# GpSimd's elementwise operations cut into four pieces each, and one weight subtraction moved to VectorE, in a fused attention and mixture-of-experts kernel

## The chip, the cores and the metric

The kernel runs on one core of one Trainium2 chip. Times are device microseconds of a whole execution. The engines are called as in the profile: PE (TensorE matmul) with PEld (its weight loads), DVE (VectorE), ACT (ScalarE), POOL (GpSimd), SP (the queue that issues most transfers).

## The reference, cut to what matters

Three layers in a row, all in float32. Attention with a causal mask over 4 batches, 8 heads, 576 positions and 64 channels is mixed, by a gate per head, with a linear memory that is read through phi(q):

```
scores = scale * q @ k^T, causal;  a = softmax(scores);  local = a @ v
phi(x) = where(x > 0, x, exp(x) - 1) + 1
mem_out = (phi(q) @ M_prev) / (phi(q) . z_prev + 1e-6)
x = g * mem_out + (1 - g) * local            # 2304 tokens of 512
```

Then routing: logits = x @ w_gate, each token goes to the one of 8 experts with the largest logit, with a factor from the softmax and a second gate. Each expert is two matrix products with a relu between (512 to 1024 to 512). A gated layer ends it: sigmoid(x @ w_gate) * (x @ w_val) @ w_out with an inner width of 1536.

## The kernel before, in words

Float32 products that need care are computed from two parts, a rounded high part (`hi`, a copy by ACT into the fp32r format) and the remainder (`lo`, a subtraction by DVE or POOL), with three matmuls for one.

**Attention** (about the first 300 us) works on 16 pairs of heads, two pairs to a group, so 8 groups. Per pair: q and k are transposed by PE and split (`q_part` L303, `k_part` L314), nine query tiles of scores are made (L345), masked with the row maximum by DVE (L365), exponentiated by ACT (L375), transposed again (L410) and multiplied with v (L440). At the end of a pair DVE turns the row sums to reciprocals (`recip`, L384 and L385), `spread` (L390, on POOL or DVE) lays them out, PE broadcasts them (L398), and DVE scales and adds (L450, L455).

**phi(q)** is computed once per group on tiles of 128 x 1152: ACT's exp, then on POOL `phi_sum` in four instructions (max L258, min L260, add L262, times z L264), on DVE `phi_norm` (a sum L269 and three tiny operations to L272), and on POOL `phi_scale` (L276). `phi_sum` of the next group cannot be far ahead, as tile `e` has one buffer and `ph` two.

**Routing** follows per batch: logits (L772), transposed (L788), copied by DVE (step `r0`, L797 and L798), argmax as a one-hot matrix (`r1`, five DVE instructions L807 to L812), factors (`r2` to `r5`, L828 to L850, on DVE or POOL with an ACT step between). For the last batch a matmul counts the tokens (`p0`, L889), a chain of 14 small DVE instructions gives each token its slot (`p1`, L896 to L973), and `p3` (L940), `p4` (L990), L996, L1000 and L1003 make the token lists. Then the first tokens are gathered (`x0`, `x1`, L1006, issued by POOL), which wait for the lists, for the store of the factors (`sd`, L853, issued by SP) and for all stores of x; the experts' first product waits for the gather.

**The first weights.** Eight parts of expert 0's weights are split while attention ends: `wh` n (L1097, ACT) and `wl` n (L1102). Parts 2 to 5 have their low part on DVE, parts 0, 1, 6 and 7 on POOL. In the kernel before, part 0 has only `wh` 0 to wait for, part 1 also `r4` of the last batch, the next ones the end of routing.

**What sets the order.** A planner (class `Plan`) simulates all steps of attention and routing with fixed costs in us, for each engine, and takes the step and the engine that can start first (rank breaks ties within 0.02 us; a step that may go to one of two engines has 0.1 added for DVE and 0.05 for POOL). A step behind one on the same engine gets a lag of 0.06 to 0.13, behind one on another engine 0.15 to 0.2. The result is written out as it stands: every engine executes its own list strictly in order, and waits there for what the others owe it. The experts and the gated layer have orders of their own that the change does not touch.

Of the kernel before, what the change touches and what calls it, by code (L numbers as in the profile page):

```python
# [9 lines left out]
F32 = mybir.dt.float32  # L10
# [3 lines left out]
ALU = mybir.AluOpType  # L14
# [4 lines left out]
P = 128  # L19
B, H, S, D = 4, 8, 576, 64  # L20
HG = 4
NP = B * H // 2
NQ = 9
NK = 5
# [5 lines left out]
NT = NTOK // P  # L30
# [24 lines left out]
class Plan:  # L55
# [15 lines left out]
    def add(self, name, rank, cost, fn, needs=(), takes=(), uses=()):  # L71

        assert name not in self.steps, name
        self.steps[name] = (rank, cost, fn, tuple(needs), tuple(takes))
        for t in (*takes, *uses):
            self.users.setdefault(t, []).append(name)
# [48 lines left out]
class Attention:  # L125
# [15 lines left out]
    def constants(self, beta):  # L141
# [41 lines left out]
        for hg in range(2):  # L183
            h0 = hg * HG
            nc.vector.tensor_copy(
                self.gf[:, hg, 0:16].rearrange("p (c h) -> p c h", h=HG),
                g[:, None, h0 : h0 + HG].to_broadcast([P, 4, HG]),
            )
# [10 lines left out]
    def load_nat(self, gi, nm, l):  # L199
        b, h0 = gi // 2, (gi % 2) * HG  # L200
        src = self.q if nm == "q" else self.k
        if l == 0:
            self.G[gi, nm] = self.ld.tile([P, 18 * 64], F32, name=f"{nm}n", tag=f"{nm}n")
        t = self.G[gi, nm]
        tv = t[:, 0:1024].rearrange("p (c h d) -> p c h d", c=4, d=64)
        for hh in (2 * l, 2 * l + 1):
            self.nc.sync.dma_start(
                out=tv[:, :, hh, :], in_=src[b, h0 + hh, 0:512, :].rearrange("(c p) d -> p c d", p=P)
            )
        self.nc.sync.dma_start(  # L210
            out=t[l * 64 : (l + 1) * 64, 1024:1152].rearrange("p (h d) -> p h d", d=64),
            in_=src[b, h0 + 2 * l : h0 + 2 * l + 2, 512:576, :].rearrange("h p d -> p h d"),
        )

    def load_z(self, gi):
        b, h0 = gi // 2, (gi % 2) * HG
        self.G[gi, "z"] = zf = self.ld.tile([P, 18 * 64], F32, name="zf", tag="zf", bufs=1)
        z1 = self.z[b, h0 : h0 + HG].rearrange("h d -> (h d)")
        for c in range(4):
            self.nc.sync.dma_start(out=zf[:, c * 256 : (c + 1) * 256], in_=z1.partition_broadcast(P))  # L220
        for l in range(2):
            self.nc.sync.dma_start(
                out=zf[l * 64 : (l + 1) * 64, 1024:1152],
                in_=z1[l * 128 : (l + 1) * 128].partition_broadcast(64),
            )
# [27 lines left out]
        self.nc.scalar.activation(self.G[gi, "e"], self.G[gi, "q"], AF.Exp)  # L253

    def phi_sum(self, gi, n):
        nc, q, ph, e = self.nc, self.G[gi, "q"], self.G[gi, "ph"], self.G[gi, "e"]
        if n == 0:
            nc.gpsimd.tensor_scalar(ph, q, 0.0, None, ALU.max)  # L258
        elif n == 1:
            nc.gpsimd.tensor_scalar(e, e, 1.0, None, ALU.min)  # L260
        elif n == 2:
            nc.gpsimd.tensor_tensor(ph, ph, e, ALU.add)  # L262
        else:
            nc.gpsimd.tensor_tensor(e, ph, self.G[gi, "z"], ALU.mult)  # L264

    def phi_norm(self, gi):
        nc = self.nc
# [5 lines left out]

    def phi_scale(self, gi):
        pv = self.G[gi, "ph"].rearrange("p (a d) -> p a d", d=64)
        self.nc.gpsimd.tensor_tensor(pv, pv, self.G[gi, "nm"][:, :, None].to_broadcast([P, 18, 64]), ALU.mult)  # L276


    GROUPS = ((0, 1, 2), (3, 4))
# [178 lines left out]
    def run(self, ex, change):  # L458
# [8 lines left out]
        add = p.add  # L467
# [8 lines left out]

        for gi in range(NP * 2 // HG):
            u0 = gi * NQ * (HG // 2)
            r = u0 - 18
            for l in range(2):  # L480
                for i, nm in enumerate("qk"):
                    add(("L", nm, gi, l), r + 2 * l + i, {"SP": 1.6}, lambda e, a=(gi, nm, l): self.load_nat(*a),
                        needs=[("L", nm, gi, 0)] * l, takes=[] if l else [(nm + "n", gi)], uses=[(nm + "n", gi)] * l)
# [7 lines left out]
            for n, c in enumerate((3.06, 3.06, 2.57, 2.57)):  # L491
                needs = [("L", "q", gi, 1)] if n == 0 else [("phe", gi)] if n == 1 else [("phs", gi, n - 1), ("phs", gi, 0)]
# [6 lines left out]

        for pi in range(NP):  # L500
            gi, u0 = pi // 2, pi * NQ
            before = [("S", u, si) for u in range(u0 - 2 * NQ, u0 - NQ) if u >= 0 for si in range(len(self.spans(ORDER[u % NQ])))]
            for g in range(2):
                n = (384, 192)[g]
                r = u0 - 13 + g
                for nm in "qk":
                    kz = nm == "k" and g == 0
                    add(("X", nm, pi, g), r, {"PE": PO + n / 1200}, lambda e, a=(nm, pi, g): self.turn(*a),
                        needs=[("L", nm, gi, pi % 2)] + (before if nm == "q" else [("X", "k", pi, 0)] if g else []),
                        takes=[("T", (nm, pi, g))] + ([("kz", pi)] if kz else []), uses=[(nm + "n", gi)])  # L510
                for j in range(2):
                    add(("qh", pi, g, j), r, {"AC": ac(n)}, lambda e, a=(pi, g, j, 0): self.q_part(*a),
                        needs=[("X", "q", pi, g)], uses=[("T", ("q", pi, g))])
                    add(("ql", pi, g, j), r, {"DV": dv(n)}, lambda e, a=(pi, g, j, 1): self.q_part(*a),
                        needs=[("qh", pi, g, j)], uses=[("T", ("q", pi, g))])
                add(("kh", pi, g), r, {"AC": ac(n)}, lambda e, a=(pi, g, 0): self.k_part(*a),
                    needs=[("X", "k", pi, g)] + ([("kh", pi, 0)] if g else []), uses=[("T", ("k", pi, g)), ("kz", pi)])
# [4 lines left out]
                    needs=[("ph", gi)] + ([("X", "ph", pi, 0)] if g else []),  # L522
                    takes=[("T", ("ph", pi, g))] + ([] if g else [("phT", pi)]), uses=[("ph", gi)])
                add(("pp", pi, g), r, {"AC": ac(n), "DV": dv(n)}, lambda e, a=(pi, g): self.p_part(e, *a),
                    needs=[("X", "ph", pi, g)] + ([("pp", pi, 0)] if g else []),
                    uses=[("T", ("ph", pi, g)), ("phT", pi)])
            kept = {}
            for n_ in range(NQ):
                u, t = u0 + n_, ORDER[n_]
                n, two = 64 * (t + 1), (pi, n_ // 2)  # L530
                sp = self.spans(t)
                for si, (k0, k1) in enumerate(sp):
                    gs = range(1 if k1 <= 384 else 2)
                    needs = [("kl", pi, g) for g in gs] + [("ql", pi, 0 if t < 6 else 1, j) for j in range(2)]
                    needs += [("S", u, 0)] if si else [("S", u - 1, len(self.spans(ORDER[(u - 1) % NQ])) - 1)] if u else []
                    add(("S", u, si), u, {"PE": PO + max(0.21 + (k1 - k0) / 2400, 3 * (k1 - k0) / 2400)}, lambda e, a=(u, si): self.scores(*a),
                        needs=needs, takes=[("Sp", (u, si))], uses=[("kz", pi)])
                    takes = [("mx", u)] + ([("Sm", two)] if n_ % 2 == 0 else []) + ([("sums", pi)] if n_ == 0 else []) if si == 0 else []
                    needs = [("S", u, si)] + ([("m", u, 0)] if si else [("m", u - 1, 0)] if n_ else [])
# [8 lines left out]
                for chunks in ([list(range(min(nb, 4)))] + ([[4]] if nb == 5 else [])):  # L548
                    f = chunks[0]
                    add(("t", u, f), u + 2, {"PE": PO + 0.107 * len(chunks)}, lambda e, a=(u, tuple(chunks)): self.turn_probs(*a),  # L550
                        needs=[("e", u), *before], takes=[("T", (u, f))], uses=[("Sm", two)])
                    for c0, c1 in ((f, min(chunks[-1] + 1, full)), (max(f, full), chunks[-1] + 1)):
                        if c0 < c1:
                            w = (c1 - c0) * 128
                            add(("v", u, c0), u + 2 + 0.1, {"AC": ac(w), "DV": dv(w)},
                                lambda e, a=(u, c0, c1, f): self.keep_probs(e, *a),
                                needs=[("t", u, f)], uses=[("T", (u, f))])
# [5 lines left out]
            for bk in range(2):  # L563
# [4 lines left out]
                    needs=[("b", pi, bk)] + ([("bc", pi, 0)] if bk else []),  # L568
                    takes=[] if bk else [("rb", pi)], uses=[("T", ("b", pi, bk))] + ([("rb", pi)] if bk else []))
            for bk in range(2):  # L570
                r = u0 + 22 + bk
                last = (2, 4)[bk]
                for i in range(last + 1):
                    needs = [("o", pi, bk, i - 1)] if i else [("L", "v", gi)]
                    needs += [k for t in range(9) if t >= 2 * i and (t <= 4 if bk == 0 else t >= 4) for k in kept[t]]
                    n = 288 - max(0, i * 128 - bk * 288)
# [3 lines left out]
                    needs=[("pp", pi, 0), ("pp", pi, 1), ("L", "M", gi), ("o", pi, bk, last)],  # L580
                    takes=[("O", ("m", pi, bk))], uses=[("MB", gi), ("phT", pi)])
                b, hp = divmod(pi, H // 2)
                first = hp == 0 and bk == 0
                add(("os", pi, bk), r + 0.5, {"DV": dv(288)}, lambda e, a=(pi, bk): self.out_scale(*a),
                    needs=[("o", pi, bk, last), ("bc", pi, bk)] + ([] if first else [("os", 4 * b, 0)]),
                    takes=[("xT", b)] if first else [], uses=[("O", (pi, bk)), ("rb", pi)] + ([] if first else [("xT", b)]))
                add(("oc", pi, bk), r + 0.5, {"DV": dv(288)}, lambda e, a=(pi, bk): self.out_add(*a),
                    needs=[("os", pi, bk), ("om", pi, bk)], uses=[("O", ("m", pi, bk)), ("xT", b)])
# [8 lines left out]
        for n, tag in enumerate(("qn", "kn", "zf", "e")):  # L597
            add(("w", 4 + n), 999, {"SP": 1.5}, lambda e, n=n: ex.load_part(self.spare(n)), needs=[("w", 3 + n), ("phs", NP * 2 // HG - 1, 3)],
                takes=[(tag, "w")])
# [6 lines left out]
        wide = [n for n in p.steps if n[0] in ("phn", "qh", "ql", "S", "m", "r", "D", "b", "t", "v", "o")]  # L606
        for n in range(8):
            add(("wh", n), 900 + n, {"AC": 0.95}, lambda e: ex.split_hi(),
                needs=[("w", 7), ("lc", B - 1, 1), *wide] + ([("wh", n - 1)] if n else []) + [("xc", NT - 1 if n else NT - 4)])
            late = [] if n < 1 else [("r4", B - 1)] if n < 2 else ["places"] if n < 5 else ["x1"]  # L610
            add(("wl", n), 900 + n, {"DV": 1.14} if n in (2, 3, 4, 5) else {"PL": 2.3},
                lambda e, n=n: ex.split_lo(n, self.nc.vector if e == "DV" else self.nc.gpsimd), needs=[("wh", n)] + late)
        for n in range(2):
            add(("f", n), 998, {"SP": 1.0}, lambda e: ex.load_part(), needs=[("wl", n)] + ([("f", n - 1)] if n else []))
        add("ahead", 999, {"SP": 3.0}, lambda e: ex.load_ahead(self.gather), needs=["x1"] + [("wl", n) for n in range(4)])
# [396 lines left out]
class Experts:  # L1012
# [84 lines left out]
        self.nc.scalar.activation(hi, t, AF.Copy)  # L1097
        self.half[n] = t, hi, lo, slot

    def split_lo(self, n, eng):  # L1100
        t, hi, lo, slot = self.half.pop(n)
        eng.tensor_tensor(lo, t, hi.bitcast(F32), ALU.subtract)  # L1102
        if slot is not None:
            self.free.append(slot)

# [579 lines left out]
```

## Time and profile before

| | us |
|---|---|
| median of 3 runs | 1127.98 |
| lowest and highest | 1125.14, 1132.57 |
| the profiled execution | 1123.5 |
| its span | 1121.7 |
| PE, PEld busy, share of the span | 92%, 80% |
| DVE, ACT, POOL busy, share of the span | 49%, 42%, 26% |

The profile describes the one execution of 1123.5 us; 1.8 us of it lie around the span. Attention fills the span to about 300 us, routing and the first gather reach to about 322, experts to about 640, the gated layer the rest.

### The profile page before, as it was taken

The numbers are of one execution on the slowest core, as the hardware profiler recorded it, in microseconds if no ns is written. First come the engines' busy times: TensorE is split into PE (matmuls) and PEld (weight loads), VectorE is DVE, ScalarE is ACT, GpSimd is POOL, SyncE is SP. The second block draws the span as 40 slices with busy tenths as digits, with TensorE's granted clock in tenths as the row PEclk, the third lists the DMA queues.
The fourth block names the chain that finished last, engine by engine and source line by source line (L and its number), as shares of the span: only waits on it lengthen the run. The fifth ranks groups of instructions, "written<-read, shape, count | busy, mean of one in ns | idle before, by whom it ended". The sixth has DMA issues, their size and how long they took to land. (4 is left out here: it accounts for less than half of the span.)

```text
span 1121.7 us, 16871 instructions
## 1 busy us (share of the span) xinstructions
PE 1037.1 (92%) x6133; PEld 900.6 (80%) x6133; DVE 545.5 (49%) x1232; ACT 466.5 (42%) x1074; POOL 293.8 (26%) x287
## 2 busy tenths in 40 slices
PE   6998998999869799979987679999999999999997
PEld 5766776777559689968976579999899999999996
DVE  6888867767585153227225699941212111121112
ACT  5875776777545252126214365521212211221211
POOL 7667245333265152025114300000110100100101
PEclk9999999999979999989998989999999999999999
DMA  5646433322268264128224466500010100100000
GB/s 119 140 103 175 83 85 85 97 61 58 66 196 291 75 210 159 38 72 280 87 62 137 141 188 197 177 12 1 29 57 1 47 10 1 58 1 1 29 1 29
DMA packets 111899, 102.50 MB, mean 91 GB/s; under 512 B 69520, under 2 KB 86928, under 8 KB 111760
## 3 DMA queue, kind: packets, MB, share of 16 engines
q1 hardware_dynamic: 107888, 88.18, 26.8%
q0 software_dynamic: 3872, 12.62, 3.7%
q8 instruction: 69, 1.13, 0.5%
q14 instruction: 70, 0.57, 0.2%
HBM read 84.49 MB, written 16.28 MB: 90 GB/s over the span
## 5 line engine op out<-in xcount | busy, mean ns | idle before, releaser
L1482 DVE TENSOR_TENSOR G<-G,pT 128x384 f32<-128x384 f32 (+1 forms) x74 | 40.1, 543 | 248.7 <-PE pT L1468 248.5
L1514 POOL DMA_INDIRECT out_dram<-o,rows x18 | 17.5, 971 | 462.7 <-ACT o L1510 213.5
L345 PE MATMUL Sp<-kz,qz 128*128 128x288 f32 (+8 forms) x480 | 100.3, 340 | 7.6 <-DVE mx L365 7.6
L1489 ACT ACTIVATE Gh<-G 128x384 fp32r<-128x384 f32 (+1 forms) x74 | 38.2, 516 | 162.3 <-DVE G L1482 162.1
L1478 ACT ACTIVATE G<-pH 128x384 f32<-128x384 f32 x72 | 35.4, 491 | 129.9 <-PE pH L1468 129.8
L345 PEld LDWEIGHTS Sp<-kz,qz 128*128 128x128 f32 x480 | 73.9, 197 | 17.0 <-DVE mx L365 9.5
L375 ACT ACTIVATE Sm<-Sm,mx 128x576 f32<-128x576 f32 (+2 forms) x144 | 79.8, 557 | 16.3 <-DVE mx L365 16.0
L1102 POOL TENSOR_TENSOR W<-raw,W 128x1024 fp32r<-128x1024 f32 x23 | 60.5, 2632 | 76.5 <-ACT W L1097 76.4
L365 DVE CUSTOM_DVE_ANT_0 Sm<-Sp,mask 128x288 f32<-128x288 f32 (+2 forms) x144 | 63.4, 450 | 18.8 <-PE Sp L345 12.4
L1499 PE MATMUL pX<-W,Gh 128*128 128x512 f32 x220 | 68.9, 394 | 0.0
L1097 ACT ACTIVATE W<-raw 128x1024 fp32r<-128x1024 f32 x60 | 61.7, 1054 | 16.9 <-DMA y_dram<-y 8.4
L283 ACT ACTIVATE pt<-T 64x128 f32<-64x128 f32 (+4 forms) x159 | 53.6, 368 | 31.9 <-PE T L410 28.2
L410 PE MATMUL T<-ident,Sm 128*128 128x128 f32 (+1 forms) x400 | 61.6, 281 | 5.0 <-ACT pt L283 3.4
L440 PE MATMUL O<-pt,vn 128*64 128x288 f32 (+4 forms) x512 | 59.5, 352 | 0.0
L1102 DVE TENSOR_TENSOR W<-raw,W 128x1024 fp32r<-128x1024 f32 x37 | 55.0, 1497 | 7.1 <-ACT W L1097 7.1
L1487 DVE TENSOR_TENSOR Gl<-G,Gh 128x384 fp32r<-128x384 f32 (+1 forms) x74 | 40.4, 546 | 33.9 <-ACT Gh L1489 33.9
L410 PEld LDWEIGHTS T<-ident,Sm 128*128 128x128 f32 (+1 forms) x400 | 43.3, 136 | 16.5 <-ACT pt L283 5.1
L1233 PE MATMUL pH<-W,xh 128*128 128x512 f32 x80 | 28.4, 501 | 28.3 <-issue 28.1
L1468 PE MATMUL pT<-xh,W 128*128 128x384 f32 x264 | 52.5, 342 | 0.0
L1468 PE MATMUL pT<-yh,W 128*128 128x384 f32 x264 | 51.3, 336 | 0.0
L440 PEld LDWEIGHTS O<-pt,vn 128*64 128x64 f32 (+1 forms) x512 | 30.4, 137 | 23.6 <-issue 11.2
L1468 PE MATMUL pH<-yh,W 128*128 128x384 f32 x240 | 46.9, 337 | 1.4 <-DVE xl L1457 1.4
(325 smaller groups left out, 2459.5 us busy)
## 6 DMA issues: line engine op xcount, KB each, us to landing
raw<-in_moe_w_dram SPq DMA_DIRECT2D x60, 512.0 KB, 4.9
raw<-in_moe_w_gate_dram SPq DMA_DIRECT2D x12, 512.0 KB, 4.3
raw<-in_moe_w_val_dram SPq DMA_DIRECT2D x12, 512.0 KB, 3.7
raw<-in_moe_w_out_dram SPq DMA_DIRECT2D x12, 512.0 KB, 3.3
y_dram<-y SPq DMA_DIRECT2D x9, 513.0 KB, 3.1
qn<-in_q_dram SPq DMA_DIRECT2D x32, 128.0 KB, 2.8
kn<-in_k_dram SPq DMA_DIRECT2D x32, 128.0 KB, 2.7
zf<-in_z_prev_dram SPq DMA_DIRECT2D x32, 128.0 KB, 5.8
```

Of the source, the lines that this page charges most:

```text
L283: self.nc.scalar.activation(out, in_, AF.Copy)
L345: nc.tensor.matmul(Sp[:, 0 : k1 - k0], lhsT=z[:, a, t, :], rhs=kz[:, c, k0:k1], start=(p_ == 0), stop=(p_ == 2))
L365: self.nc.vector.tensor_tensor_reduce(out=self.Sm[u][:, k0:k1], in0=self.Sp[u, si][:, 0 : k1 - k0], in1=self.mask[:, 512 - 64 * t + k0 : 5 ...
L375: self.nc.scalar.activation(self.Sm[u], self.Sm[u], AF.Exp, scale=-1.0, bias=self.mx[u][:, si : si + 1], accum_out=self.sums[pi][:, ORDER[ ...
L410: nc.tensor.transpose(T[:kr, n * 128 : (n + 1) * 128], self.Sm[u][:, i * 128 : i * 128 + kr], self.ident)
L440: nc.tensor.matmul(O[j * 64 : (j + 1) * 64, q0 - q0b : 288], lhsT=self.G[gi, "v"][:kr, i, 2 * l + j, :], rhs=PT[:kr, j, i, q0:q1], start=( ...
L1097: self.nc.scalar.activation(hi, t, AF.Copy)
L1102: eng.tensor_tensor(lo, t, hi.bitcast(F32), ALU.subtract)
L1468: nc.tensor.matmul(t, lhsT=w[:, k * P : (k + 1) * P], rhs=x[:, k, :], start=(m == k == 0), stop=(m == 2 and k == 3),)
L1482: nc.vector.tensor_tensor(t, t, p, ALU.mult)
L1487: nc.vector.tensor_tensor(l, t, hi.bitcast(F32), ALU.subtract)
L1499: nc.tensor.matmul(po[g][jj], lhsT=a[:, ts], rhs=w, start=(f == 0 and m == 0), stop=(f == NF - 1 and m == 2), skip_group_check=True,)
```

## The change

The four instructions of `phi_sum` and the one of `phi_scale` are issued as four each, over 320, 320, 256 and 256 of the 1152 columns. `wl` 1, on POOL, is issued as four instructions of 256 columns. `wl` 0 goes from POOL to DVE, in one instruction. `wh` 0 no longer names the last logits copy as a need. The planner's costs for all of these but `wl` 0 (2.3 on POOL before, 1.14 on DVE after) stay as they were. `wl` 6 and 7 and the experts' splits stay whole.

```
+PIECES = ((0, 5), (5, 10), (10, 14), (14, 18))
 def phi_sum(self, gi, n):
-    nc, q, ph, e = self.nc, self.G[gi, "q"], self.G[gi, "ph"], self.G[gi, "e"]
-    if n == 0:
-        nc.gpsimd.tensor_scalar(ph, q, 0.0, None, ALU.max)
...
+    for a, b in PIECES:
+        q, ph, e = (self.G[gi, nm][:, a * 64 : b * 64] for nm in ("q", "ph", "e"))
+        if n == 0:
+            nc.gpsimd.tensor_scalar(ph, q, 0.0, None, ALU.max)
+        elif n == 1:
+            nc.gpsimd.tensor_scalar(e, e, 1.0, None, ALU.min)
+        elif n == 2:
+            nc.gpsimd.tensor_tensor(ph, ph, e, ALU.add)
+        else:
+            nc.gpsimd.tensor_tensor(e, ph, self.G[gi, "z"][:, a * 64 : b * 64], ALU.mult)
 def phi_scale(self, gi):
-    self.nc.gpsimd.tensor_tensor(pv, pv, self.G[gi, "nm"][:, :, None].to_broadcast([P, 18, 64]), ALU.mult)
+    for a, b in PIECES:
+        nm = self.G[gi, "nm"][:, a:b, None].to_broadcast([P, b - a, 64])
+        self.nc.gpsimd.tensor_tensor(pv[:, a:b], pv[:, a:b], nm, ALU.mult)
 # Attention.run
-    needs=[("w", 7), ("lc", B - 1, 1), *wide] + ([("wh", n - 1)] if n else []) + [("xc", NT - 1 if n else NT - 4)])
+    needs=[("w", 7), *wide] + [("lc", B - 1, 1)] * (n > 0) + ([("wh", n - 1)] if n else []) + [("xc", NT - 1 if n else NT - 4)])
-    add(("wl", n), 900 + n, {"DV": 1.14} if n in (2, 3, 4, 5) else {"PL": 2.3},
-        lambda e, n=n: ex.split_lo(n, self.nc.vector if e == "DV" else self.nc.gpsimd), needs=[("wh", n)] + late)
+    add(("wl", n), 900 + n, {"DV": 1.14} if n in (0, 2, 3, 4, 5) else {"PL": 2.3},
+        lambda e, n=n: ex.split_lo(n, *((self.nc.vector, 1) if e == "DV" else (self.nc.gpsimd, 4 if n < 2 else 1))), needs=[("wh", n)] + late)
-def split_lo(self, n, eng):
+def split_lo(self, n, eng, parts=1):
     t, hi, lo, slot = self.half.pop(n)
-    eng.tensor_tensor(lo, t, hi.bitcast(F32), ALU.subtract)
+    w = 1024 // parts
+    for o in range(0, 1024, w):
+        eng.tensor_tensor(lo[:, o : o + w], t[:, o : o + w], hi.bitcast(F32)[:, o : o + w], ALU.subtract)
```

## Rows read from the trace of the kernel before

**Rows 1.** Windows: stretch, length, busy us by engine, clock, DMA share, GB/s.
```profile
38.00:46.00 8.00, 6.83 (x49) 5.06 (x50) 7.13 (x17) 5.14 (x18) 7.13 (x3) 1.00 0.66 143
62.00:72.00 10.00, 7.83 (x50) 5.95 (x47) 6.10 (x12) 4.84 (x17) 6.85 (x5) 0.83 0.35 83
82.00:88.00 6.00, 4.72 (x38) 3.65 (x35) 5.19 (x9) 3.31 (x10) 6.00 (x2) 1.00 0.78 146
106.00:120.00 14.00, 10.02 (x63) 7.85 (x61) 13.42 (x33) 6.76 (x20) 9.47 (x4) 0.88 0.29 97
180.00:192.00 12.00, 8.42 (x50) 6.76 (x48) 11.67 (x27) 5.37 (x17) 8.24 (x3) 0.86 0.21 68
```

**Rows 2.** Three source lines: min/median/max ns, first and last start.
```profile
L384 DVE TENSOR_SCALAR rc<-sums,iog x16: 223/230/3044, 26.2 to 285.6; 128x9 f32<-128x9 f32 x16
...
L390 DVE TENSOR_TENSOR dg<-rows,rc x2: 3056/3221/3386, 62.0 to 82.2; 128x576 f32<-128x576 f32 x2
...
L844 DVE TENSOR_SCALAR r_a<-r_a x2: 1395/1464/1534, 114.1 to 187.0; 128x4 f32<-128x4 f32 x1, 128x5 f32<-128x5 f32 x1
```

**Rows 3.** Timeline of DVE and POOL, 106 to 114: start, us, instruction.
```profile
107.07 3.12 POOL L260 TENSOR_SCALAR e<-e 128x1152 f32<-128x1152 f32 x1
...
107.39 2.64 DVE L812 TENSOR_TENSOR O<-r_t,r_vm 128x32 fp32r<-128x32 f32 x1
...
110.27 0.18 DVE L828 TENSOR_TENSOR r_d<-L,r_mx 128x32 f32<-128x32 f32 x1
110.28 2.65 POOL L262 TENSOR_TENSOR ph<-ph,e 128x1152 f32<-128x1152 f32 x1
...
110.37 2.61 DVE L832 TENSOR_TENSOR r_sel<-O,L 128x32 f32<-128x32 f32 x1
```

**Rows 4.** Timeline of POOL, 84 to 95: the instruction behind an L258.
```profile
84.84 3.39 POOL L260 TENSOR_SCALAR e<-e 128x1152 f32<-128x1152 f32 x1
```

**Rows 5.** Groups of POOL instructions by form: busy, mean ns, idle before.
```profile
L258 POOL TENSOR_SCALAR ph<-qn 128x1152 f32<-128x1152 f32 x8 | 25.0, 3127 | 6.9 <-PE T L299 5.1 <-DMA MB<-in_M_prev_dram 1.8
L262 POOL TENSOR_TENSOR ph<-ph,e 128x1152 f32<-128x1152 f32 x8 | 21.1, 2640 | 0.4
...
L276 POOL TENSOR_TENSOR ph<-ph,nm 128x1152 f32<-128x1152 f32 x8 | 17.0, 2120 | 30.6 <-DVE nm L272 19.6 <-DVE mx L365 7.4 <-DMA vn<-in_v_dram 3.6
L390 POOL TENSOR_TENSOR dg<-rows,rc 128x576 f32<-128x576 f32 x14 | 16.1, 1153 | 72.5 <-PE T L398 55.3 <-DVE pt L285 8.8 <-DVE rb L285 3.3
L940 POOL TENSOR_SCALAR Bm<-col,rf,tok 128x128 fp32r<-128x128 f32 x8 | 6.2, 794 | 1.1 <-DVE sid L850 1.1
...
L844 POOL TENSOR_SCALAR r_d<-r_d 128x5 f32<-128x5 f32 x1 | 0.3, 279 | 0.1
```

**Rows 6.** Timeline of DVE: the first and the fourth sum of `phi_norm`.
```profile
31.98 1.35 DVE L269 TENSOR_REDUCE nm<-e 128x18 f32<-128x1152 f32 x1
...
97.38 1.35 DVE L269 TENSOR_REDUCE nm<-e 128x18 f32<-128x1152 f32 x1
```

**Rows 7.** Timeline of all engines, routing of the last batch to the gather.
```profile
301.32 2.35 POOL L1102 TENSOR_TENSOR W<-raw,W 128x1024 fp32r<-128x1024 f32 x1 [12.33 <-ACT W L1097]
301.35 2.38 DVE L808 TENSOR_TENSOR r_t<-L,r_mx 128x40 f32<-128x40 f32 x1
...
304.23 0.23 DVE L812 TENSOR_TENSOR O<-r_t,r_vm 128x40 fp32r<-128x40 f32 x1
...
305.06 0.45 DVE L896 TENSOR_TENSOR_SCAN inc<-seg,T 128x144 f32<-128x144 f32 x1
...
306.84 2.33 DVE L915 CAST ranki<-rank 128x18 int32<-128x18 f32 x1
...
310.61 0.37 SPq L853 DMA_DIRECT2D x_dram<-sid  x1
...
314.26 1.12 POOL L1006 DMA_INDIRECT xn<-x_dram,kept  x1 [5.13 <-DVE starts L983]
...
335.79 1.21 DVE L1102 TENSOR_TENSOR W<-raw,W 128x1024 fp32r<-128x1024 f32 x1
```

More of the change, by code (lines that the diff above doesn't have):

```diff
@@ L255, in phi_sum @@
     def phi_sum(self, gi, n):
-        nc, q, ph, e = self.nc, self.G[gi, "q"], self.G[gi, "ph"], self.G[gi, "e"]
-        if n == 0:
-            nc.gpsimd.tensor_scalar(ph, q, 0.0, None, ALU.max)
[L259 to L264, printed above, removed]
+        nc = self.nc
+        for a, b in PIECES:
[8 more added lines that the diff above has]
+                nc.gpsimd.tensor_tensor(e, ph, self.G[gi, "z"][:, a * 64 : b * 64], ALU.mult)
     def phi_norm(self, gi):
```

## The prediction, on record before the change was run

> **What bounds the kernel now.** The page's busy times come first: PE is busy 92% of the span (table above), so time is to be gained only where PE has nothing to do or runs at its low clock. The windows show where in attention that is. In five stretches, 50 us together, PE is busy 6.83 of 8, 7.83 of 10, 4.72 of 6, 10.02 of 14 and 8.42 of 12 us [rows 1]: 1.17, 2.17, 1.28, 3.98 and 3.58, in sum 12.2 us idle. In the same stretches DVE and POOL are both nearly full. In the second, fourth and fifth the granted clock is 0.83, 0.88 and 0.86 of full speed on average [rows 1]; what is missing, times the length, is 1.7 us each, 5.1 us. Part of that fell while PE had no work; I take 4 as lost. So 16.2 us of attention are at stake.
>
> The source lines and the timeline then say what DVE does there. A reciprocal's first step that takes 0.23 us at the median took 3.04 once, and both outlays on DVE took over 3 us [rows 2], although the same 128x576 product takes the slower POOL 1.15 [rows 5]. At 107.39 a product of 32 columns takes 2.64 us; POOL's 3.12 us operation runs from 107.07 [rows 3]. The DVE operation ends at 110.03, POOL's at 110.19. At 110.28 the next POOL operation begins, and the DVE operation at 110.37 takes 2.61 and ends at 112.98, POOL's at 112.93. So a DVE operation with two SBUF inputs, or a plain one from SBUF to SBUF, stands still until POOL's running operation is about done, and all that is queued behind it on DVE (masks, copies out of PSUM) with it; PE runs dry after 1 to 3 us. In routing the same happens twice on the path to the first gather: 2.38 us at 301.35 and 2.33 at 306.84 for operations of 40 and 18 columns [rows 7], where a sibling takes 0.23 [rows 7].
>
> **The change, part by part.** *Pieces against the stalls.* What a DVE operation waits for becomes one piece, if it is let in between two pieces. The rows say it is: L812 got in between two POOL operations of which the second reads what the first wrote [rows 3]; the outlay of 82.19 (3.06 us, ends 85.25) got in between L258 and L260, which don't depend on each other, and L260 took 3.39 instead of 3.12 [rows 2, 4]. A tensor_tensor piece of 320 columns is some 0.25 + 320 x 2.1 ns = 0.9 us, so a wait is at most about 0.9, and lowest nothing. The lone stalls (38 to 46, 62 to 72, 82 to 88) waited 2.8, 2.7 and 2.4 us (3.04 less 0.23; 3.39 and 3.06 less some 0.7 of their own) and left PE idle for 1.17, 2.17 and 1.28 [rows 1, 2]: PE bridged 1.6, 0.5 and 1.1. With at most 0.9 of waiting only the second can leave something; of 4.6 us I take 4.4 as gone. The stretches at 106 and 180 hold a chain of eight such operations each (r1 to r4 of a batch). In the first the three long waits (2.64, 2.61 and 1.53 less 0.2 each) sum to 6.2 us against 3.98 idle [rows 1 to 3], so PE bridges some 2.2; the other, with 3.58 idle, holds the other long L844 [rows 2] and is taken as its like. With pieces each waits between 0.3 (half of a piece, when POOL streams at all) and 0.75; I take 0.5, for the row of L828, which slipped through without waiting while L832 behind it waited [rows 3]: 8 x 0.5 = 4, less 2.2, leaves 1.8 idle each, 3.6 together (0.4 to 7.6 by the ends). The clock fell after idle times of 2.17 and more and did not after 1.28 [rows 1], so the 4 us come back. Of 16.2 us this leaves 12.4.
>
> *What pieces cost POOL.* Each added instruction costs POOL its fixed part. A tensor_scalar of 5 columns takes 0.28 [rows 5]; the form with two per-row scalars at 128 columns takes 0.79, which less 128 x 2.5 ns is 0.47. Below, 0.15, since two products of 576 and 1152 columns (1.15 and 2.12) extrapolate to 0.19 at none and neighbours overlap a little. I take 0.25, nearest to the plain form. Fifteen more per group are 3.75 us (2.3 to 7.0), 30 us over eight groups. Eight groups spread over 300 us, and the first four phi_norms lie within 65 [rows 6], so the later groups have more room, and POOL's idle time takes it in (19.6 of the 30.6 us before L276 are waits for DVE, and 72.5 us lie before the outlays [rows 5]). Before 100 us it matters: from one phi_norm to the next POOL owes L276, two tensor_scalars, two tensor_tensors and an outlay, 2.12 + 2 x 3.13 + 2 x 2.64 + 1.15 = 14.8 [rows 5], and DVE about 2.1 with latencies 0.3: 17.2 us. The first and the fourth phi_norm are 65.4 us apart [rows 6], 21.8 each; with 3.75 more the chain is 20.95, so the fourth comes at best 2.6 us earlier, while the lone stalls give back 4.4 plus some 1.3 of clock by then. DVE, in order, waits at phi_norm for the rest, with masks and copies behind it; PE bridges about half: 1.5 us off. Attention gains 10.9.
> [...]
>
> *The first weights' low part.* The planner's list, followed by hand with its costs: `wh` 0 starts as before (the logits copy it no longer names is long done), so `wl` 0 can start when `r1` ends, 0.13 before DVE could do `r2` and before the counts are there. It goes on DVE between `r1` and `p1`, 1.21 us [rows 7]. POOL, now empty, gets `r2`, and later `r4` and `wl` 1 behind it. On the chip: L808 loses 2.18, so L812's end moves from 304.46 to about 302.3; `wl` 0 fills DVE to 303.5; L896 starts 1.5 us earlier than 305.06 and L915 runs free (2.1 more): `p1` is 3.6 earlier. But `r2` on POOL waits for `wl` 0's reads, `r3` stands behind a `wh` more on ACT, and `r4` ends near 308, so the factors' store goes at about 308.4 against 310.61. Then `wl` 1 in four pieces (2.35 + 3 x 0.25) occupies POOL to about 312, with the gather behind it: 312 against 314.26. 2.2 us gained; bounds 4.3 (both stalls) and -1 (POOL's factor steps later still). SP gains no instruction; the second raw load, tied to `wl` 1, goes some 1 us later, and is for expert 1, which is split only beside expert 0's products. The `wh` edit alone costs nothing.
>
> The sum is 10.9 + 2.2 = 13.1: 1110.4 against the profiled 1123.5. That execution was 4.5 faster than the median shown; from the median it is **1115**.
>
> **The rivals.** *Blocked in turn (0.22).* Each of the eight chained operations waits for a whole piece, 8 x 0.8 = 6.4, as much as before. The chains keep their idle time and clock; the lone stalls give 5.7, less 1.5, routing 2.2: 6.4 us, 1122. For it speaks L832, held at once by the next POOL operation; against it that L828 passed [rows 3].
> [...]
> *POOL sets the early pace (0.16).* With 0.35 us and more per added instruction the chain is 22.5 us, and nothing of the first 100 us is gained: 13.1 less 4.2, 8.9 us, 1119. For it speaks the 0.79 us row, against it the 0.28 one.
> *Slower (0.06).* The same chain at 0.7 us per added instruction: 27.7 against 21.8, three times, 17.7 us late at the fourth phi_norm, against 8.9 from the chains and routing: 1137. It turns from gain to loss at about 0.5 (24.7, 8.7 us late); no row has so high a fixed part.
> *Not what stretches them (0.06).* The long DVE operations wait for something else, and pieces change nothing: 1128. Their ends within 0.2 us of POOL's speak against it.
>
> **How the numbers follow.** The forecast has 0.50; its own range is 1109 to 1120. This kernel's timing tells no change below about 1%, 11.3 us. Faster by that: most of the forecast (0.44) and a quarter of the early-pace case (0.04), 0.48; slower 0.06; within it 0.46. The range is 1106 (all idle and clock back, both stalls of routing, the median's spread) to 1124 (blocked in turn with nothing from routing).
>
> **What would show it.** The windows at 106 and 180 with PE idle under 2 us and full clock; L384 and the outlays on DVE under 1.2 us; L812 and L832 under 1. Spacing of POOL's pieces tells the fixed part, 0.25 or more; phi_norm's fourth sum near 95. One L1102 on DVE right behind L812 near 302.3, the gather near 312 less what attention gained. Wrong if chained operations each take a piece's time, if DVE stands idle before L269, or if the gather stands behind the factors' store.

## The result, and the profile after

The changed kernel takes **1113.35 us** (median of six runs, 1111.45 to 1114.58) against 1128.41 (1125.14 to 1132.57) for the kernel before in the same runs: ratio 0.9861, 95% interval 0.9838 to 0.9884. It is 1.4% faster. The forecast was 1115 in a range of 1106 to 1124, with faster by over 1% as its likeliest sign. Line numbers from phi(q) on are 3 to 7 higher than before (L384 is L389, L390 is L395, L812 is L817, L1006 is L1011).

The profiled execution after is the slowest of its six (1114.58), the one before (1123.5) lies below all six of its own. So the two traces differ by only 8.9 us of span. The marks in the traces say where they part:

| us from the span's start | before | after | gained since the mark above |
|---|---|---|---|
| last tokens of x complete (first of the eight last x transposes, L868, now L873) | 298.52 | 288.33 | 10.19 |
| first gather (L1006, now L1011) | 314.26 | 301.93 | 2.14 |
| first transposes of the gated layer (L1450, now L1457) | 644.3 | 631.8 | 0.2 |
| end | 1121.7 | 1112.8 | -3.6 |

The last row lies in a layer that the change doesn't touch; the last section returns to it. Attention and the way to the gather gave 12.3 us; both had been put close to that (10.9 and 2.2).

The page's busy times of the kernel after:
```profile
PE 1038.6 (93%) x6133; PEld 903.0 (81%) x6133; DVE 521.3 (47%) x1229; ACT 466.6 (42%) x1074; POOL 312.8 (28%) x415
```
POOL is busy for more of the span (28%, before 26%). The windows of attention, columns as in [rows 1]:
```profile
20.00:30.00 10.00, 8.49 (x52) 7.34 (x49) 6.69 (x24) 8.10 (x27) 7.94 (x11) 0.83 0.64 146
38.00:46.00 8.00, 7.97 (x58) 5.76 (x55) 5.92 (x20) 6.07 (x21) 8.00 (x10) 1.00 0.81 146
62.00:72.00 10.00, 10.00 (x75) 7.70 (x71) 6.16 (x20) 7.86 (x24) 10.00 (x14) 1.00 0.58 121
82.00:88.00 6.00, 6.00 (x42) 4.61 (x41) 5.41 (x18) 4.65 (x15) 6.00 (x8) 1.00 0.92 229
100.00:120.00 20.00, 15.70 (x97) 13.46 (x96) 11.46 (x47) 10.94 (x34) 12.61 (x16) 0.83 0.60 156
172.00:180.00 8.00, 8.00 (x62) 7.19 (x61) 7.07 (x30) 5.81 (x16) 7.98 (x10) 1.00 0.34 114
180.00:192.00 12.00, 12.00 (x89) 9.41 (x88) 9.60 (x30) 9.97 (x31) 7.48 (x11) 1.00 0.54 139
```
The three stretches with lone stalls [rows 1] are full and at full clock, though POOL has not a free moment in them. So is the second chain, which now runs from 174 to 180. Of these stretches only 20 to 30 and the one around 106 have PE idle and the clock down, the latter with 4.3 of 20 us idle.

The DVE operations that had been held [rows 2, 3], min/median/max ns in the kernel after:
```profile
L389 DVE TENSOR_SCALAR rc<-sums,iog x16: 222/230/850, 27.4 to 275.4; 128x9 f32<-128x9 f32 x16
...
L395 DVE TENSOR_TENSOR dg<-rows,rc x2: 753/754/755, 61.6 to 78.1; 128x576 f32<-128x576 f32 x2
...
L849 DVE TENSOR_SCALAR r_a<-r_a x2: 183/318/454, 103.9 to 178.2; 128x4 f32<-128x4 f32 x1, 128x5 f32<-128x5 f32 x1
```
Where 3.04, 3.39 and 1.53 us stood, no operation takes over 0.85. The second chain's timeline, with POOL working without a break from 172.02 to 185.27:
```profile
174.78 0.45 DVE L813 TENSOR_TENSOR r_t<-L,r_mx 128x40 f32<-128x40 f32 x1
175.26 0.20 DVE L814 TENSOR_TENSOR r_t<-r_t,desc 128x40 f32<-128x40 f32 x1
...
175.72 0.39 DVE L817 TENSOR_TENSOR O<-r_t,r_vm 128x40 fp32r<-128x40 f32 x1
...
176.50 0.19 DVE L833 TENSOR_TENSOR r_d<-L,r_mx 128x40 f32<-128x40 f32 x1
176.61 0.46 DVE L837 TENSOR_TENSOR r_sel<-O,L 128x40 f32<-128x40 f32 x1
...
178.22 0.18 DVE L849 TENSOR_SCALAR r_a<-r_a 128x5 f32<-128x5 f32 x1
```
Each waits 0 to 0.27 us beyond its own 0.18 to 0.2, where 0.5 had been taken.

What stopped PE near 106 is another thing. Each tile of 128 tokens of x is copied out of PSUM into one of two buffers `xt`, which SP then stores. SP's queue in the kernel after:
```profile
92.00 1.75 SPq L221 DMA_DIRECT2D zf<-in_z_prev_dram  x4
...
95.03 3.56 SPq L244 DMA_DIRECT2D vn<-in_v_dram  x4
99.42 2.52 SPq L247 DMA_DIRECT2D vn<-in_v_dram  x1
102.03 1.99 SPq L235 DMA_DIRECT2D MB<-in_M_prev_dram  x2
...
104.76 0.85 SPq L888 DMA_DIRECT2D x_dram<-xt  x2
```
The copies into `xt` on ACT's timeline, the same stretch:
```profile
100.72 0.60 ACT L288 ACTIVATE xt<-T 128x512 f32<-128x512 f32 x1 [0.23 <-PE T L873]
...
101.63 0.60 ACT L288 ACTIVATE xt<-T 128x512 f32<-128x512 f32 x1
...
110.19 0.60 ACT L288 ACTIVATE xt<-T 128x512 f32<-128x512 f32 x1 [5.01 <-DMA x_dram<-xt]
```
The first two tiles are copied by 102.23, but SP issues their stores only at 104.76, behind loads for the next group; the first of these (z) could not go before 92.00, because POOL's last piece of L267 reads the old z until 91.97. The third copy finds both buffers still waiting for their stores, ACT stands for 5.01 us, and PE waits 4.30 us, from 106.55 to 110.85, for ACT's next copy. This is a new wait that none of the prediction's parts had. In the kernel before SP issues the same two stores here:
```profile
106.86 1.23 SPq L883 DMA_DIRECT2D x_dram<-xt  x2
```
There the first copy ends at 106.83, so its store goes at once. With the change the copy is 5.5 us earlier and its store only 2.1. That z's wait for POOL sets the whole delay is read from the queue's order; no run moved the z load alone.

Routing of the kernel after, as in [rows 7]:
```profile
291.86 0.23 DVE L817 TENSOR_TENSOR O<-r_t,r_vm 128x40 fp32r<-128x40 f32 x1
291.98 1.22 DVE L1109 TENSOR_TENSOR W<-raw,W 128x1024 fp32r<-128x1024 f32 x1
292.17 1.17 POOL L837 TENSOR_TENSOR r_sel<-O,L 128x40 f32<-128x40 f32 x1 [0.69 <-DVE O L817]
...
293.33 0.45 DVE L901 TENSOR_TENSOR_SCAN inc<-seg,T 128x144 f32<-128x144 f32 x1
...
295.11 0.17 DVE L920 CAST ranki<-rank 128x18 int32<-128x18 f32 x1
...
298.29 0.37 SPq L858 DMA_DIRECT2D x_dram<-sid  x1
...
298.80 2.79 POOL L1109 TENSOR_TENSOR W<-raw,W 128x256 fp32r<-128x256 f32 x4
...
301.93 1.13 POOL L1011 DMA_INDIRECT xn<-x_dram,kept  x1 [0.34 <-DVE kept L989]
```
The order is the forecast one: `wl` 0 on DVE right behind `r1`, `r2` on POOL held beside it (L837 takes 1.17 us and ends 0.14 behind `wl` 0, where another on POOL, at 243.8, takes 0.26; that it is `wl` 0's reads that hold it is not shown), the cast free (0.17 for 2.33), then the factors' store, `wl` 1 in four pieces and the gather behind it, 13.60 us after attention's mark instead of 15.74.

### The profile page after: what moved, and what is told of

Same layout as the page of the kernel before. It is cut to its first block, busy times and chain, and to the rows that moved or that the text cites. A ratio compares the mean times of both kernels' runs of the same rounds, so it can differ in the third digit from the quotient of the medians.

```text
span 1112.8 us, 17008 instructions
## 1 busy us (share of the span) xinstructions
PE 1038.6 (93%) x6133; PEld 903.0 (81%) x6133; DVE 521.3 (47%) x1229; ACT 466.6 (42%) x1074; POOL 312.8 (28%) x415
## 5 line engine op out<-in xcount | busy, mean ns | idle before, releaser
L1109 POOL TENSOR_TENSOR W<-raw,W 128x1024 fp32r<-128x1024 f32 (+1 forms) x25 | 58.6, 2349 | 64.7 <-ACT W L1102 64.6
L445 PEld LDWEIGHTS O<-pt,vn 128*64 128x64 f32 (+1 forms) x512 | 29.9, 135 | 23.5 <-issue 10.9
```

The lines of the kernel that those rows point to most:

```text
L445: nc.tensor.matmul(O[j * 64 : (j + 1) * 64, q0 - q0b : 288], lhsT=self.G[gi, "v"][:kr, i, 2 * l + j, :], rhs=PT[:kr, j, i, q0:q1], start=( ...
L1109: eng.tensor_tensor(lo[:, o : o + w], t[:, o : o + w], hi.bitcast(F32)[:, o : o + w], ALU.subtract)
```

## The experiments

All were timed in five rounds; ratios are to the kernel before in the same runs. Edits are against the changed kernel.

**e1: only `phi_sum` in pieces** (`phi_scale`, `wl` 0, `wl` 1 and `wh` 0 as before):
```
 def phi_scale(self, gi):
-    for a, b in PIECES:
+    for a, b in ((0, 18),):
 # Attention.run
-    needs=[("w", 7), *wide] + [("lc", B - 1, 1)] * (n > 0) + ...
+    needs=[("w", 7), ("lc", B - 1, 1), *wide] + ...
-    {"DV": 1.14} if n in (0, 2, 3, 4, 5) ... 4 if n < 2 else 1
+    {"DV": 1.14} if n in (2, 3, 4, 5) ... 1
```


> Only the four instructions of phi_sum are in pieces; phi_scale is whole, and the first weights are as in the kernel before. Theory (a DVE operation that needs the shared path stands still until POOL's running instruction is done): attention's gain is all here, since the long waits fell under phi_sum's instructions: the last eight transposes of x begin near 288 instead of 298.5, the two waits of over 2.1 us in routing stay, and the time is about 2 us above that of the whole change: 1116 against 1128. Rival (the consumers of phi_scale start earlier on its pieces): most of the gain is missing, 1124 or more.

Measured 1116.09 (1112.47 to 1118.76), ratio 0.9879 [0.9847, 0.9911]. The lone stalls and the second chain's are gone without the rest of the change; the gap of PE near 106 is there too (3.06 us), and so is one wait beside the whole `phi_scale` (an L389 of 1.22 us). Attention's mark is at 285.13. In routing both long operations are back, and the gather comes 16.15 us after the mark:
```profile
287.96 2.38 DVE L813 TENSOR_TENSOR r_t<-L,r_mx 128x40 f32<-128x40 f32 x1
...
293.45 2.32 DVE L920 CAST ranki<-rank 128x18 int32<-128x18 f32 x1
```

**e2: only the weights' part** (`phi_sum` and `phi_scale` whole):
```
-        for a, b in PIECES:
+        for a, b in ((0, 18),):
```


> phi_sum and phi_scale are whole; only the first weights' low parts are as in the change (part 0 on DVE, part 1 in four pieces on POOL). Theory: attention is as before, with its long waits; routing's path to the gather is 2 us shorter: about 1126, ratio 0.998. Rival (the gain of the change is routing's and what follows it): 1118 or less.

Measured 1125.55 (1122.09 to 1130.97), ratio 0.9976 [0.9954, 0.9998]. Attention is as before, with PE busy 16.01 of 20 us in 100 to 120 and 8.42 of 12 in 180 to 192. The gather comes 13.90 after attention's mark, 1.84 less than before. So the two parts add: about 12 and 3 us of the 15, and e1's and e2's intervals cover that.

**e3: a third x buffer**, to take the new wait away. The tile for every third early copy lies in a buffer that is idle until the gather:
```
-            xt = self.r2.tile([P, DM], F32, name="xt", tag="xt")
+            xt = self.xn[0][:, :DM] if j < EARLY and j % 3 == 2 else self.r2.tile([P, DM], F32, name="xt", tag="xt")
```


> The change, with a third buffer for the tiles of x that wait for their store (every third tile before the thirteenth lies in a buffer that is idle until the gather). Theory (at 105 to 110 ACT waits 5.0 us for a store of x to land, which the SP queue issued late behind the z load that waits for POOL's last product, and this takes the place of the stall removed there): the wait goes, PE's idle time of 4.3 us between 100 and 120 falls under 1.5 and the low clock after it goes: 1108 to 1109, 4 to 5 us under the change. Rival (another wait is due there next, as POOL's pace sets the groups): no faster than the change by more than 1 us, 1113.

Measured 1108.63 (1100.41 to 1112.24), ratio 0.9814 [0.9776, 0.9852]. The window around 106 with this edit:
```profile
100.00:120.00 20.00, 20.00 (x149) 16.04 (x147) 16.63 (x60) 15.39 (x49) 14.26 (x19) 1.00 0.94 168
```
PE is full there, the clock never falls, and the time is the expected one. Four pieces had freed DVE here too; the gain had gone into the wait for a buffer.

**e8: the first four x stores from ACT's queue**, two buffers as before:
```
-        self.nc.sync.dma_start(out=self.x_dram[j * P : (j + 1) * P, :DM], in_=self.xt[j])
+        (self.nc.scalar if j < 4 else self.nc.sync).dma_start(out=self.x_dram[j * P : (j + 1) * P, :DM], in_=self.xt[j])
```


> The change, with the first four stores of x issued by ACT's queue right after the copies, instead of by SP, where they stand behind the loads of z, v and M. If SP's order delays them (copies done at 101.3 and 102.2, stores issued at 104.8), they go 2.5 to 3 us earlier, ACT's wait of 5.0 us falls to 2 to 3 and the time by 2 to 4 us: 1109 to 1111. If only the transfer itself is slow there (5 us to land with the DMA engines full), or ACT pays for the issues, no gain: 1113.

Measured 1105.91 (1103.08 to 1110.49), ratio 0.9808 [0.9778, 0.9839], more than expected. ACT's copy and queue in this kernel:
```profile
99.65 0.60 ACT L288 ACTIVATE xt<-T 128x512 f32<-128x512 f32 x1 [0.23 <-PE T L873]
...
101.27 0.35 ACTq L888 DMA_DIRECT2D x_dram<-xt  x1
...
105.34 0.60 ACT L288 ACTIVATE xt<-T 128x512 f32<-128x512 f32 x1 [0.21 <-DMA x_dram<-xt]
```
The first store goes 1.0 us behind the end of its copy, where SP's went 3.4 behind, and the third copy waits 0.21 instead of 5.01. So most of the wait was SP's late issue; the rest is that the store also lands sooner behind it (4.1 us for 5.4, from the store's issue to the third copy). Two buffers are enough.

**e4: `wl` 0 on POOL in four pieces**, not on DVE:
```
-    {"DV": 1.14} if n in (0, 2, 3, 4, 5) else {"PL": 2.3}
+    {"DV": 1.14} if n in (2, 3, 4, 5) else {"PL": 2.3}
```


> The change, but part 0's low part stays on POOL, in four pieces. If cutting is what helps routing, no wait of DVE there is above 0.8 us, the 1.2 us of part 0 are off DVE, and the gather is no later than in the change: 1112 to 1114. If moving it to DVE is what helps (POOL's pieces hold DVE's small operations one after the other), the gather is 1 to 2 us later: 1115.

Measured 1115.31 (1110.21 to 1119.67), ratio 0.9881 [0.9848, 0.9915]; the times don't tell it from the change. The trace does:
```profile
289.26 2.78 POOL L1109 TENSOR_TENSOR W<-raw,W 128x256 fp32r<-128x256 f32 x4 [12.32 <-ACT W L1102]
289.28 0.76 DVE L813 TENSOR_TENSOR r_t<-L,r_mx 128x40 f32<-128x40 f32 x1
...
290.07 0.65 DVE L814 TENSOR_TENSOR r_t<-r_t,desc 128x40 f32<-128x40 f32 x1
...
291.33 0.76 DVE L833 TENSOR_TENSOR r_d<-L,r_mx 128x40 f32<-128x40 f32 x1
...
294.26 0.70 DVE L920 CAST ranki<-rank 128x18 int32<-128x18 f32 x1
```
The four pieces hold one operation each: the three shown up to L833 and, for 0.44 us, L817; L837 behind them finds POOL free, and the cast waits for a piece of `wl` 1. That is near to what the rival "blocked in turn" had said of all chains. The gather comes 14.89 after the mark, 1.3 later than with the change. Moving `wl` 0 to DVE, with the order that the planner then gives, is worth that much in these two traces.

**e5 and e6: two pieces, and nine**
```
-PIECES = ((0, 5), (5, 10), (10, 14), (14, 18))
+PIECES = ((0, 9), (9, 18))                              # two
+PIECES = tuple((a, a + 2) for a in range(0, 18, 2))     # nine
```


> The change with two pieces of 576 columns in phi instead of four. Theory (DVE waits for the piece that runs): single waits up to 1.7 us, the batch chain near 180 is held three to four times for about 1.2 us, PE idles there for 1 to 3 us again; POOL's chain is 0.8 us a group shorter. Attention ends 2 to 5 us later than in the change: 1115 to 1118. Rival (any cut frees DVE, since one gap is enough): no later, 1113.

> The change with nine pieces of 128 columns. If waits are what counts, each is under 0.5 us and the time is at or under the change, 1111 to 1113. If POOL's pace counts too, 25 more instructions per group at the 0.15 us that four pieces cost (3.6 instead of 3.12 us) are 3.8 us, POOL's part from one phi_norm to the next grows from 19.5 to 23 us, the fourth sum of phi_norm moves from 92 to over 100, and the time is 4 to 9 us above the change: 1117 to 1122.

Two pieces: 1109.97 (1108.37 to 1114.92), ratio 0.9857 [0.9826, 0.9888]. Nine: 1123.87 (1118.71 to 1127.28), ratio 0.9956 [0.9931, 0.9982]. The first expectation was wrong: two pieces are no slower than four, no L389 takes over 0.92, one other operation takes 1.33 (L851), and the gap between the two is enough. Part of why they do so well is another wait: the third copy into `xt` waits 1.81 us here, where it waits 5.01 with four pieces. Nine pieces are slower than the 1122 expected at most. The expected cause is there: POOL's chain is too slow, and DVE's sum of `phi_norm` waits for it at its second and third turn (1.83 and 3.41 us). But one operation also stood far longer than any piece lasts:
```profile
79.69 1.35 DVE L272 TENSOR_REDUCE nm<-e 128x18 f32<-128x1152 f32 x1 [3.41 <-POOL e L267]
...
94.50 3.77 POOL L265 TENSOR_TENSOR ph<-ph,e 128x128 f32<-128x128 f32 x9
...
96.70 5.33 DVE L389 TENSOR_SCALAR rc<-sums,iog 128x9 f32<-128x9 f32 x1
...
98.22 3.79 POOL L267 TENSOR_TENSOR e<-ph,zf 128x128 f32<-128x128 f32 x9
```
L389 ends at 102.03, with the last of POOL's 18 products (102.01). It was let in at none of some twelve boundaries between pieces.

**e11 and e12: nine pieces for the products alone, and for the scalars alone**, to see which pieces shut DVE out:
```
 def phi_sum(self, gi, n):
-        for a, b in PIECES:
+        for a, b in PIECES if n < 2 else NINTHS:     # products: phi_scale in NINTHS too
+        for a, b in NINTHS if n < 2 else PIECES:     # scalars
```


> Only the tensor_tensor steps (the sum, the product with z, the scaling) in nine pieces of 128 columns, the two tensor_scalar steps in four. With nine pieces everywhere one L389 on VectorE stood 5.33 us, from 96.70 to 102.03: through the rest of one chain of nine tensor_tensor pieces and the whole of the next, which ended at 102.01. Theory A (gap): tensor_tensor pieces of 128 columns leave VectorE no way in, so the run of nine holds it like one long operation; here an L389, a layout or a product of routing's steps will again take over 2 us beside such a run, and the time is 1117 to 1124. Theory B (pace): only the number of instructions counts; 15 more than with four pieces a group, about 2 us per group, nothing held over 1 us, 1114 to 1119.

> The reverse: the two tensor_scalar steps in nine pieces, the tensor_tensor steps in four. Theory A (gap): nothing is held over 1 us behind the products; the pace costs 10 instructions a group, some 1.7 us, 1113 to 1117. Theory B (pace): by the number of instructions a little less than the reverse, the same 1113 to 1117. If instead tensor_scalar pieces are what held, this is the slow one, 1118 or more, with an L389 or a layout over 2 us beside a run of nine L263.

Products in nine: 1118.15 (1116.83 to 1119.74), ratio 0.9908 [0.9875, 0.9941]. Scalars in nine: 1114.70 (1110.62 to 1118.81), ratio 0.9876 [0.9836, 0.9916]. Both times lie in both theories' ranges; the traces tell more. The first has the long hold again, as theory A said (5.08 us from 90.87). The second has it too, against a chain of products in pieces of 320 and 256 columns:
```profile
88.31 3.07 POOL L266 TENSOR_TENSOR ph<-ph,e 128x320 f32<-128x320 f32 x4
...
89.67 4.75 DVE L390 TENSOR_SCALAR rc<-sums,iog 128x9 f32<-128x9 f32 x1
...
91.33 3.06 POOL L268 TENSOR_TENSOR e<-ph,zf 128x320 f32<-128x320 f32 x4
...
94.82 1.15 POOL L396 TENSOR_TENSOR dg<-rows,rc 128x576 f32<-128x576 f32 x1 [0.42 <-DVE mx L371]
```
(These two kernels' lines are one higher.) L390 ends at 94.42, POOL's last product at 94.39: six boundaries passed it by. So the width of the pieces is not the reason, and theory A falls with its 128 columns; so does theory B's word that nothing is held over 1 us. Its pace fits both times, which don't single it out. In the changed kernel the same operation, begun at 88.95 beside the first piece of L267, was let in after that piece (0.85). That POOL's next piece can win a boundary is shown; what decides who wins it is open.

**e7, e9 and e10: combinations.** The third buffer with `phi_scale` whole; the third buffer with two pieces; the store from ACT with two pieces and `phi_scale` whole:

> The third buffer for x, and phi_scale in one instruction (phi_sum and the first weights in pieces as in the change). phi_scale's pieces cost POOL 0.43 us a group and DVE was held by it only once before (1.0 us at 57.6). If POOL's pace still counts, 0.5 to 1.5 us under the third buffer alone: 1107 to 1108. If not, the same within noise, 1109.

> Two pieces instead of four, with the third x tile. Open is why two pieces were as fast as four (1109.97 against 1113.35). Theory A: only because their order of transfers let the first x store go earlier (the third copy waited 1.81 us there and 5.01 with four pieces); with that wait gone for both, POOL's saving and DVE's longer waits of up to 0.9 us cancel, and two pieces give what four give with the third tile, 1108 to 1112. Theory B: two pieces are better in themselves, since POOL has 10 instructions a group less; then it is 1103 to 1106, and the third copy's wait plays no part.

> Two pieces for phi_sum, phi_scale whole, the first four x stores from ACT's queue: the pieces that paid, put together. If the gains of the single steps add (two pieces about 3 below four, the store from ACT 7 below), it is 1100 to 1104. If they are the same gain taken twice (all of them take away the one stall near 106), it is 1104 to 1108, no better than the store from ACT alone.

Measured 1105.56 (1105.06 to 1108.06), ratio 0.9808 [0.9781, 0.9835]; 1105.50 (1104.10 to 1107.92), ratio 0.9806 [0.9777, 0.9834]; and 1108.16 (1105.21 to 1114.81), ratio 0.9822 [0.9793, 0.9851]. No interval parts these from e3 and e8. Whether two pieces are better in themselves is not settled: the second is at theory B's number, but its attention mark (282.86) is later than e3's (280.26). The gains don't add: e10 is no better than the store from ACT alone. All of them mend the one stretch near 106: from 100 to 120 PE is busy all 20.00 us in e7 and e9, and 18.55 at a clock of 0.91 in e10. These kernels, at 1106 to 1108, beat the kernel before by some 2% and the changed one by about half a per cent (ratios of 0.981 to 0.982 against 0.986). The intervals of e7 and e9 lie just below the change's, that of e8 touches it, and those of e3 and e10 overlap it.

The `wh` 0 edit was not run: with the old need put back, the planner's order is the same on every engine.

## Why the prediction was right, and where only its sum was

**The mechanism held.** e1 and e2 show it in both places: with the long POOL operations whole, DVE operations beside them take up to 3.4 us; in the changed kernel, with all of these in pieces, none of the short ones up to the gather takes over 0.85. That the two engines share a path, as e1's theory has it, no run shows; shown are the holds. Nor is every operation from SBUF to SBUF held: in the kernel before, the reciprocal L385 at 58.90 (0.22 us) and the sum L818 at 185.92 (0.20 us) ran inside POOL's L258 and L264. PE's idle time goes with them, but for the gap near 106. The rivals "not what stretches them" (1128) and "slower" (1137) are out, and "blocked in turn" (1122) is what e4's routing shows, but not what the chains of the changed kernel do.

**The lone stalls** (4.4 of 4.6 us idle, and their clock) came back as forecast: 4.6 us of idle time and the 1.7 of clock in 62 to 72. (That PE runs dry after 1 to 3 us is not what the prediction's own working gives: 1.6, 0.5 and 1.1.)

**The chains' residual, 1.8 each, was the step that failed**, in both directions. In the second nothing is left: the operations waited 0 to 0.27 instead of 0.5, and three of the six shown passed at once (POOL's pieces beside them were tensor_scalars; whether that is why wasn't tried). In the first the 2.2 us that were to come back, and the clock, did not. From 100 to 120 PE was busy 16.02 us at clock 0.91 before and 15.70 at 0.83 after, about 1.9 us worse (an estimate from these windows, which hold somewhat different work). DVE's operations there were as quick as elsewhere (0.35, 0.50 and 0.45 for L817, L837 and L849); the store waited behind SP's loads. The prediction asked which stall goes and stopped; it followed POOL's and DVE's queues, but not SP's, whose z load waits for POOL's last piece. e3 and e8 put this wait at 5 to 7 us by their medians, and it was the largest single error.

**POOL's price per added instruction, 0.25, was too high.** Four pieces last 3.60 for 3.12, 3.05 for 2.64 and 2.55 for 2.12 us: 0.14 to 0.16 for each added instruction, and with nine (4.46, 3.79, 3.27) 0.14 to 0.17. That is the lower bound, the extrapolation of 0.15 from two lengths of the same operation, and not the 0.28 us of a tiny one; neighbouring pieces overlap by only 0.03 to 0.08 us, which is too little to explain the difference. The rival in which POOL sets the early pace, at 0.35 and more, is out with it. The sums of `phi_norm` show it:
```profile
92.01 1.35 DVE L272 TENSOR_REDUCE nm<-e 128x18 f32<-128x1152 f32 x1
```
It is the fourth and comes 5.4 us earlier than [rows 6], where 2.6 was the best foreseen; the spacing is 19.7 us for 21.8, and by the working's own chain 17.2 + 15 x 0.15 = 19.5. From the first to the fourth sum 6.4 us are gained, more than the 5.7 that the lone stalls and their clock were to give, so nothing of the 1.5 us taken off for the pace was due.

**The total was right by luck: these errors cancel.** Windows before and after give: lone stalls 4.6 + 1.7, the second chain 3.6 + 1.7, the first chain -1.9, and a clock of 0.83 at 20 to 30, which before doesn't have, some -1.4: 8.3 of the 10.2 us. The other 1.9 the windows don't resolve. The low clock at 20 to 30 is not the change's: e3, e4 and e8, with the same instructions up to there, are granted 1.00. It also speaks against the prediction's reading that the clock fell after 2.17 us of idle time and more and not after 1.28: here it fell at a single gap of 1.20 us; a gap of 1.21 at the same place of the kernel before left it at 1.00, as did one of 2.68 in the kernel after, some 14 us earlier. What decides it is open.

**Routing's 2.2 was right in its sum** (2.14; e2 1.84), and in its order. e4 says what part is the move to DVE: 1.3 us.

## What to carry to other kernels

Where a short VectorE operation takes ten times its median (here 3.04 us for 0.23), look whether its end falls on the end of a long GpSimd operation; cutting that in two cost 0.12 to 0.15 us in e5 (3.26 for 3.12, 2.76 and 2.80 for 2.64) and freed nearly all (no L389 over 0.92), cutting it in nine cost most of the gain (1123.87). Before a stall is booked as gain, follow every queue of the stretch one step further, the transfers' too: here a store queued behind loads that waited for GpSimd took the place of one of five stalls (ACT's 5.01 us). And a right total can hide two wrong terms, so check it window by window.

## What the runs showed that was not expected

GpSimd shut out a waiting VectorE operation at six or more boundaries in a row (4.75 us in e12, 5.08 in e11, 5.33 in e6), with pieces of 128 as of 320 columns. In e6 and e12 it ended with the last of a whole run of instructions (102.03 and 102.01, 94.42 and 94.39); at 88.95 in the changed kernel the same operation got in after one piece (0.85 us).

The gated layer, which nothing here touches, takes 477.4 to 481.3 us from its first transposes to the end in the profiled executions of these kernels. The layer begins at 631.8 in the kernel after and at 644.3 in the one before. Two windows of after, then three of before:
```profile
632.00:640.00 8.00, 7.31 (x29) 6.91 (x29) 6.00 (x11) 4.81 (x8) 0.00 (x0) 0.56 0.64 203
656.00:664.00 8.00, 6.93 (x21) 6.36 (x22) 6.98 (x15) 3.50 (x6) 0.00 (x0) 0.57 0.47 154
```
```profile
644.00:652.00 8.00, 7.04 (x36) 6.66 (x37) 5.59 (x11) 5.57 (x9) 0.00 (x0) 0.80 0.52 184
652.00:660.00 8.00, 5.21 (x30) 4.92 (x28) 7.91 (x16) 5.14 (x11) 0.00 (x0) 0.84 0.85 222
668.00:676.00 8.00, 7.34 (x39) 6.93 (x40) 7.96 (x18) 4.22 (x8) 0.00 (x0) 1.00 0.56 184
```
Both executions enter the layer at a granted clock of 0.50 (632 to 634 after, 644 to 646 before). Before is back at full after some 3 us, falls again at a gap of PE of 2.78 us (652 to 660), and stays at full through the next, of 2.44. After needs some 7 us, stays at full through two gaps of 1.19 and 1.23 us, and falls at the next, of 3.01. Over four windows of 8 us the missing share of the clock, times the length, is some 7.0 us after and 3.4 before; that is about the difference of the layer's times.

e1, e3, e10 and e11 take as long as after (480.9 to 481.3), e2, e4, e5, e9 and e12 as long as before or nearly (477.4 to 477.9), and e6, e7 and e8 lie between. Each kernel has only one trace, so it isn't shown that no edit has a part in this; the set doesn't go by what the edits do. So one execution's trace can hold 3.6 us that no edit is shown to cause, and the two traces compared here do. With them back the difference is 12.5 us; the other 2.6 of the medians' 15.1 are in no trace shown.
